# A gated-attention kernel with routed rows: VectorE's order in a step, the place of the score transposes, gate loads, and the first chunk's M

## The chip, the cores and the metric

The kernel runs on one core of a Trainium2 chip. A core has five engines that run side by side, each with its own queue in program order: TensorE (PE in the profile; PEld are its weight loads), VectorE (DVE), ScalarE (ACT), GpSimd (POOL) and SyncE (SP), which here only issues DMAs. TensorE writes into PSUM; VectorE and ScalarE read it there. The metric is the device time of one execution in microseconds, as the median over runs.

## The reference

Two blocks, one behind the other. The first is an mLSTM cell over four batches, eight heads, 768 time steps and 40 elements to a head; the second picks 128 of the 768 rows of each batch by a score and sends them through a two-layer network.

```python
for t in range(S):                                   # per batch and head
    m_new = max(f[t] + m, i[t])
    C = exp(f[t] + m - m_new) * C + exp(i[t] - m_new) * outer(v[t], k[t])
    n = exp(f[t] + m - m_new) * n + exp(i[t] - m_new) * k[t]
    m = m_new
    y[t] = sigmoid(o[t]) * (C @ q[t]) / max(abs(n @ q[t]), 1)
x = y as rows of 320                                 # heads side by side
scores = x @ w_gate
top = the 128 rows of a batch with the largest scores
out[top] = x[top] + sigmoid(scores[top]) * (relu(x[top] @ w1) @ w2);  out elsewhere = x
```

## The kernel before

**Chunks and steps.** The time steps of a batch are cut into six chunks of 128, so there are 24 steps, numbered n = 0 to 23; step n treats chunk c = n mod 6 of batch b = n div 6. Within a chunk the recurrence becomes matrix products: scores of keys with queries (`pS`), multiplied by decay weights (`W`) to give `P`, and `P` times the values (`pH`); the state `C` from the chunks before contributes through `pIC`. The order on every engine is the order in which the program writes the operations (a manual schedule); waits for data and for free buffers are added to it.

**The gates.** The sums of f and the running maxima M are made for three chunks at a time (group g = 0 and 1) on 96 rows: `sums`, `maxima`, `ends` (three matmuls `pe`), `carry` (the state m from chunk to chunk), `carried` (three matmuls `pm`), `level` (M with the carried m), `scales` (`wk`, `r`) and `columns`/`keep` (`pc`, `cols`). M and a are each split into three bf16 parts (`split`), from which `operands(u, c)` builds, for the batches 2u and 2u+1 and chunk c, two operands: six small matmuls into two PSUM tiles `pO`, then `a_o` by ScalarE and `M_o` either by VectorE (`beside=True`, one operation) or by ScalarE (four operations). `weights` multiplies the two (`pW`) and takes the exponential to give `W`; `causal` masks W on GpSimd.

**A step.** `step(n)` issues, in this order: the loads of chunk n + 4; `within(n)` (`pH`); `exchange(n + 1)` (`pIC`), `decay` (GpSimd) and `products(n + 1)` (`pS`); `weights(n + 2)`; `norm` (VectorE adds `pH` to `num` and makes the denominators `den` and `rec`; GpSimd makes `sor`); `compare(n - 1)` (VectorE, `ge`); `result` (VectorE: `x`, and `scr`, which sums the score into `sc`; the store of x); fillers (`warm`) or the layers of the network; `turned(n + 2)` (transposes `pt`, copied to `T` by ScalarE); `gated` (ScalarE, tanh and add on `so`); `causal` and `stated` (`wv`) on GpSimd; `spread(n)` (transpose `pb` of the score just made, copied to `sb` by ScalarE); in some steps `operands`; and last `weighted(n + 1)` (VectorE, `P`) and `exchanged(n + 1)` (VectorE, `num` and `C`). In the first steps the order differs a little: W is made for other chunks, and the second group of gates is worked off between.

**What is shared.** PSUM is tight. `pt` and `pW` (and, in the changed kernel, `pg`) share two buffers; `pb`, `pO`, `pe`, `pm`, `pc` and the tiles of the ranking and the network share two; `pH` and the fillers `pw` share one; `pIC` has one.

**Ranking.** From `compare` come counts of how many rows of a batch have a larger score; in the next batch's first step they become ranks and a selection, in its second the chosen rows are gathered, and from its third on they go through the two layers.

**Loads.** k, q, v and o of a chunk are four DMAs of 160 KB on SP's queue into one of five sets of buffers. Their padding columns are written once at the start (`pads`).

## Time and profile before

| | |
|---|---|
| median of 14 runs | 203.68 us (201.86 to 205.34) |
| profiled execution | 203.21 us |
| its span | 201.5 us |
| TensorE busy, weight loads | 180.3 us (90%), 147.2 us (73%) |
| VectorE, ScalarE, GpSimd busy | 143.9, 103.6, 99.6 us (71%, 51%, 49%) |
| DMA | 24.37 MB, 121 GB/s over the span |

The span runs from the first to the last instruction that the profile shows; the profiled execution's own time is 1.71 us longer. Busy time of an engine that others wait for is what counts; idle time elsewhere costs nothing. TensorE's busy time can contain slow stretches: the profile gives the granted clock for each stretch.

### The profile page before, as it was taken

The numbers are of one execution on the slowest core, as the hardware profiler recorded it, in microseconds if no ns is written. First come the engines' busy times: TensorE is split into PE (matmuls) and PEld (weight loads), VectorE is DVE, ScalarE is ACT, GpSimd is POOL, SyncE is SP. The second block draws the span as 40 slices with busy tenths as digits, with TensorE's granted clock in tenths as the row PEclk, the third lists the DMA queues.
The fourth block names the chain that finished last, engine by engine and source line by source line (L and its number), as shares of the span: only waits on it lengthen the run. The fifth ranks groups of instructions, "written<-read, shape, count | busy, mean of one in ns | idle before, by whom it ended". The sixth has DMA issues, their size and how long they took to land.

```text
span 201.5 us, 6516 instructions
## 1 busy us (share of the span) xinstructions
PE 180.3 (90%) x2597; PEld 147.2 (73%) x2606; DVE 143.9 (71%) x418; ACT 103.6 (51%) x245; POOL 99.6 (49%) x148
## 2 busy tenths in 40 slices
PE   6988979969779779799999999899999998998990
PEld 2556858856648648698988789788887897978970
DVE  7649997867477667578688689967886899576101
ACT  5684467794784685664644445456445554201110
POOL 7149708526296375426555766266557661122201
PEclk9999999997999999999999999999999999999999
DMA  4999999999969999977899679778993101010100
GB/s 81 108 171 142 157 173 162 187 224 123 207 135 145 218 172 202 160 125 108 125 146 159 125 127 153 126 131 108 150 135 80 37 33 36 33 37 29 36 0 33
DMA packets 105854, 24.37 MB, mean 121 GB/s; under 512 B 100640, under 2 KB 105248, under 8 KB 105824
## 3 DMA queue, kind: packets, MB, share of 16 engines
q1 hardware_dynamic: 105296, 22.60, 73.9%
q0 software_dynamic: 384, 1.31, 2.0%
q8 instruction: 20, 0.33, 0.8%
q14 instruction: 10, 0.08, 0.2%
q10 hardware_dynamic: 144, 0.05, 0.1%
HBM read 19.37 MB, written 4.59 MB: 119 GB/s over the span
## 4 chain that ended last, share of the span: by engine, by line
PE 51%; DVE 19%; issue 9%; ACT 7%; DMA 5%; SPq 4%; POOL 3%; POOLq 1%
PE pH L385 11%; PE pS L328 8%; PE pt L286 6%; PE ph L496 5%; PE pIC L354 5%; PE py L505 3%; ACT T L287 3%; DVE P L334 3%; PE pIC L360 3%; PE pW L306 3%; POOL sor L400 3%; PE pw L178 3%; DVE scr L408 3%; DVE x L405 2%; SPq L93 2%
## 5 line engine op out<-in xcount | busy, mean ns | idle before, releaser
L400 POOL TENSOR_TENSOR sor<-so,rec 128x320 f32<-128x320 f32 x24 | 23.4, 976 | 47.8 <-DVE rec L398 46.3
L307 ACT ACTIVATE W<-pW 128x512 f32<-128x512 f32 x48 | 26.1, 596 | 39.4 <-PE pW L306 15.5
L312 POOL TENSOR_SCALAR_AFFINE_SELECT W<-W 128x512 f32<-128x512 f32 x48 | 33.2, 715 | 16.6 <-ACT W L307 16.2
L287 ACT COPY T<-pt 128x512 f32<-128x512 f32 x48 | 26.0, 591 | 18.7 <-PE pt L286 18.6
L334 DVE TENSOR_TENSOR P<-pS,W 128x512 f32<-128x512 f32 x48 | 30.7, 679 | 0.8 <-POOL W L312 0.8
L385 PE MATMUL pH<-v,P 128*64 128x64 f32 x768 | 28.7, 228 | 1.4 <-DVE P L334 1.4
L385 PEld LDWEIGHTS pH<-v,P 128*64 128x64 f32 x768 | 25.2, 139 | 5.3 <-DVE P L334 2.4
L328 PE MATMUL pS<-T 64*128 64x128 f32 x384 | 28.1, 286 | 0.0
L286 PE MATMUL pt<-ident,qk 128*128 128x128 f32 x192 | 25.7, 275 | 0.3 <-DMA qk<-in_q_dram 0.3
L286 PEld LDWEIGHTS pt<-ident,qk 128*128 128x128 f32 x192 | 21.9, 141 | 5.0 <-ACT W L307 1.3
L328 PEld LDWEIGHTS pS<-T 64*128 64x128 f32 x384 | 23.5, 189 | 1.5 <-issue 0.2
L496 PE MATMUL ph<-xeT,w 128*128 128x128 f32 x192 | 23.8, 280 | 0.0
L496 PEld LDWEIGHTS ph<-xeT,w 128*128 128x128 f32 x192 | 22.1, 192 | 1.7 <-issue 1.6
L392 DVE TENSOR_TENSOR num<-num,pH 128x328 f32<-128x328 f32 x20 | 9.9, 496 | 18.3 <-PE pH L385 18.2
L405 DVE TENSOR_TENSOR x<-num,sor 128x320 f32<-128x320 f32 x20 | 11.9, 594 | 10.3 <-POOL sor L400 10.3
L505 PE MATMUL py<-w,hT 128*128 128x320 f32 x64 | 19.1, 440 | 0.0
L319 POOL TENSOR_TENSOR wv<-v,cols 128x328 f32<-128x328 f32 x20 | 15.0, 751 | 5.1 <-DVE cols L260 5.1
L354 PE MATMUL pIC<-C,T 128*64 128x82 f32 x320 | 15.8, 242 | 0.8 <-DVE C L377 0.8
L421 DVE SCALAR_TENSOR_TENSOR ge<-sb,sc,earlier 128x128 bf16<-128x128 f32 (+5 forms) x23 | 16.5, 715 | 0.0
L408 DVE CUSTOM_DVE_ANT_0 scr<-x,wg 128x320 f32<-128x320 f32 x24 | 14.6, 608 | 0.8
L354 PEld LDWEIGHTS pIC<-C,T 128*64 128x64 f32 x320 | 13.2, 141 | 2.2 <-issue 1.7
L247 ACT ACTIVATE M_o<-pO,of_which,which 128x128 bf16<-128x128 f32 x36 | 13.5, 457 | 2.2 <-PE pO L236 1.4
(131 smaller groups left out, 260.4 us busy)
## 6 DMA issues: line engine op xcount, KB each, us to landing
qk<-in_k_dram SPq DMA_DIRECT2D x24, 160.0 KB, 3.8
qk<-in_q_dram SPq DMA_DIRECT2D x24, 160.0 KB, 4.6
v<-in_v_dram SPq DMA_DIRECT2D x24, 160.0 KB, 4.9
so<-in_o_gate_dram SPq DMA_DIRECT2D x24, 160.0 KB, 4.8
out_dram<-x SPq DMA_DIRECT2D x24, 160.0 KB, 1.9
w<-in_moe_w_dram SPq DMA_DIRECT2D x2, 640.0 KB, 4.4
w<-in_moe_w_dram SPq DMA_DIRECT2D x2, 512.0 KB, 3.8
w<-in_moe_w_dram SPq DMA_DIRECT2D x1, 256.0 KB, 3.9
```

What stands on the lines that cost most here:

```text
L286: nc.tensor.transpose(pt[:, p, :], qk[:, j, 2 * p:2 * p + 2, :].rearrange("s a d -> s (a d)"), ident)
L287: nc.scalar.copy(out=T[:, j], in_=pt)
L307: nc.scalar.activation(out=W[:, h0:h0 + 4, :], in_=pW, func=AF.Exp)
L312: nc.gpsimd.affine_select(out=W[:, h0:h0 + 4, :], in_=W[:, h0:h0 + 4, :], compare_op=OP.is_ge, fill=0.0, base=0, pattern=[[0, 4], [1, L]], ...
L328: nc.tensor.matmul(pS[j][:, p, :], T[e, 0, p, :], T[e, 1, p, :], start=True, stop=True)
L334: nc.vector.tensor_tensor(out=P[:, :, j, :], in0=pS[j], op=OP.mult, in1=W.rearrange("p (n a) t -> p n a t", a=2)[:, :, j, :])
L354: nc.tensor.matmul(pI[t, 2 * p * D1:2 * (p + 1) * D1], T[:, 1, p, t], C[:, p].rearrange("e a d -> e (a d)"), start=True, stop=True)
L385: nc.tensor.matmul(pH[t, 2 * p + j, :], P[:, p, j, t], v1[:, 2 * p + j, :], start=True, stop=True)
L400: nc.gpsimd.tensor_tensor(out=sor, in0=so, in1=rec.unsqueeze(2).to_broadcast([128, H, D]), op=OP.mult)
L408: nc.vector.tensor_tensor_reduce(out=scr, in0=x, in1=wg, scale=1.0, scalar=0.0, op0=OP.mult, op1=OP.add, accum_out=sc[:, c:c + 1])
L496: nc.tensor.matmul(self.ph[:, f % 4, :], w1[:, j, f * 128:(f + 1) * 128], self.xeT[:, j, :], start=(j == 0), stop=(j == NDC - 1))
L505: nc.tensor.matmul(self.py, self.hT[:, f, :], w2[:, f, :], start=(f == 0), stop=(f == NFC - 1))
```

## The change

1. **Order of VectorE in a step.** Behind the denominators come `exchanged(n + 1)` and `weighted(n + 1)` (in step 0 `weighted` first), ahead of `compare` and `result`. `weights`, `causal` and `stated` for chunk n + 2 and the layers follow `norm` in the program; `gather` stands behind the layers, `columns_of` and the entry of the layers behind the transposes.
2. **Scores a step later.** `spread(n - 1)` and `compare(n - 1)` are both issued in step n: spread behind the transposes and ahead of `gated`, compare behind `result`. In a batch's first step (and in the last step of all) spread comes right behind `pS` and compare ahead of `result`.
3. **Operands.** `operands` stands at the end of a step, in steps 1 and 2 for the chunks 4 and 5, in steps 3 to 8 for the second pair of batches. Where `beside` is false the two `pO` tiles are one.
4. **Gate loads.** Each of the four gate tensors is one DMA instead of three; three of them are on ScalarE's queue. The row `w_gate` is loaded once (1 x 320) and spread to 128 rows by a matmul with a column of ones (`pg`), instead of a 160 KB DMA.
5. **First chunk's M.** Before the first chunk there is no state, so the running maximum needs no carry there: the three parts of M for chunk 0 are made from it at once, on 32 rows, and `operands(0, 0)` uses them; `level` and the split of all 96 rows follow.
6. **Start.** `pH(0)` is issued before step 0, ahead of the second half of chunk 1's transposes, `pW(1)` and `pIC(0)`. Padding columns of chunks 0 and 1 are written by ScalarE, those of 2, 3 and 4 by GpSimd; a's first split moves to GpSimd; the second group's sums and maxima stand ahead of the state's copy.

```diff
     def load_gates(eng, dst, src, g):
-        for c in range(3):
-            t = slice((3 * g + c) * L, (3 * g + c + 1) * L)
-            eng.dma_start(out=dst[g][c * BH:(c + 1) * BH], in_=src[:, :, t].rearrange("b h p -> (b h) p"))
+        t = slice(3 * g * L, 3 * (g + 1) * L)
+        eng.dma_start(out=dst[g], in_=src[:, :, t].rearrange("b h (c p) -> c (b h) p", p=L))
...
-        pO = [ps_m.tile([128, L], FP, name=f"pO{j}", tag="m") for j in range(2)]
+        if beside:
+            pO = [pool.tile([128, L], FP, name=f"pO{j}", tag=tag) for j in range(2)]
+        else:
+            both = pool.tile([128, 2, L], FP, name="pO", tag=tag)
+            pO = [both[:, j] for j in range(2)]
...
+        soon = n > 0 and (c == 0 or n == N - 1)
         if n + 1 < N:
+            decay(*steps[n + 1])
+            if n == 0:
+                pS[n + 1] = products(T[n + 1])
             give = exchange(*steps[n + 1], loaded[n + 1][0], T[n + 1], wv[n + 1])
-            decay(*steps[n + 1])
-            pS[n + 1] = products(T[n + 1])
-        if 1 < n < NT - 2:
-            operands(0, n + 2, beside=False)
-        if n + 2 < N and not late:
-            W[n + 2] = weights(*steps[n + 2])
+            if n > 0:
+                pS[n + 1] = products(T[n + 1])
+        if soon:
+            pb, pc = steps[n - 1]
+            spread(pc, *state[pb][1][:2])
 
         num, sor = norm(nums.get(n), pH, so)
...
-        if n > 0:
-            pb, pc = steps[n - 1]
+        if n == 0:
+            P[n + 1] = weighted(pS[n + 1], W[n + 1])
+        if n + 1 < N:
+            nums[n + 1] = exchanged(*steps[n + 1], *give)
+        if 0 < n < N - 1:
+            P[n + 1] = weighted(pS[n + 1], W[n + 1])
+        if soon:
             compare(pc, *state[pb][1])
         if c == 0:
             state[b] = open_batch()
-        result(b, c, num, sor, state[b][0])
...
+        run(more.get("weights", ()))
+        if n + 2 < N:
+            if n != 1:
+                stated(n + 2)
+            W[n + 2] = weights(*steps[n + 2])
+            causal(W[n + 2])
+        layer(b, c)
+        if b > 0 and c == 1:
+            picked[b - 1] = gather(b - 1, number(sel[b - 1], token))
+        if n + 2 < N:
+            turned(n + 2)
...
+        if n > 0 and not soon:
+            pb, pc = steps[n - 1]
+            spread(pc, *state[pb][1][:2])
         if n + 2 < N:
-            turned(n + 2)
             gated(n + 2)
...
+        result(b, c, num, sor, state[b][0])
+        if n > 0 and not soon:
+            compare(pc, *state[pb][1])
...
+        if n in (1, 2):
+            operands(0, n + 3, beside=False)
+        elif 3 <= n < 3 + NT:
+            operands(1, n - 3, beside=False)
```

and at the start (the hooks of steps 0 and 1 are listed where they are passed):

```python
    def second_operands():
        split(1, 1, nc.gpsimd)
        operands(0, 2, beside=False)
        ends(1)

    def level_and_split():
        level(1, kept["pm"])
        scales(1)
        split(1, 0, nc.vector)

    def more_operands():
        operands(0, 3)
        kept["pc"] = columns(1)

    step(0, pH=pH, carry=[sums_and_state], weights=[second_operands], end=[lambda: carry(1), second_places])
    step(1, carry=[lambda: kept.update(pm=carried(1))], sor=[level_and_split], weights=[more_operands],
         end=[lambda: keep(1, kept["pc"])])
```

## The prediction

> **What bounds the kernel now.** I read the page's busy times first, then the list of waits, then timelines at TensorE's longest gaps, then windows of one microsecond for the granted clock.

> ```profile
> PE 180.3 (90%) x2597; PEld 147.2 (73%) x2606; DVE 143.9 (71%) x418; ACT 103.6 (51%) x245; POOL 99.6 (49%) x148
> ```

> ```profile
> DVE num L392 <- PE pH L385: 18.2, 14, 2.7
> ...
> DVE x L405 <- POOL sor L400: 12.1, 20, 0.6
> ...
> PE pO L236 <- ACT sb L415: 6.6, 5, 1.7
> ...
> PE pH L385 <- DVE P L334: 1.4, 4, 0.5
> ```

> TensorE is busy 90% of the span, so only its idle time and its slow-clock time can be won. VectorE waits for TensorE (18.2 us for pH), while TensorE waits for P only 1.4 us in all. The diff's main idea, P earlier, therefore attacks a wait that hardly exists. The large entry is pO waiting for ScalarE's copy of sb. One such place, from the timeline (start, duration, engine, line, tiles, in brackets the idle time before):

> ```profile
> 50.73 0.27 PE L414 MATMUL pb<-ident,sc 128*128 128x128 f32 x1
> ...
> 50.94 0.34 PE L236 MATMUL pO<-a,placea 32*128 32x128 bf16 x3
> ...
> 51.41 0.47 ACT L297 ACTIVATE so<-so 128x320 f32<-128x320 f32 x1
> 51.92 0.47 ACT L298 ACTIVATE so<-so 128x320 f32<-128x320 f32 x1
> 52.29 0.25 ACT L415 COPY sb<-pb 128x128 f32<-128x128 f32 x1
> 52.59 0.32 PE L236 MATMUL pO<-M,placeM 32*128 32x128 bf16 x3 [1.32 <-ACT sb L415]
> ```

> pb and the two pO tiles share two PSUM buffers. The second pO needs pb's buffer, and pb's copy stands on ScalarE behind tanh and add. TensorE stops for 1.32 us, and pH of the next step stands behind it. Steps 3, 4, 5, 7 and 8 show 1.65, 1.32, 0.90, 1.32 and 1.37 us, 6.56 in sum. After the longest the clock falls (last three columns: clock, DMA share, GB/s):

> ```profile
> 42.00:43.00 1.00, 0.02 (x1) 0.00 (x0) 1.00 (x3) 0.97 (x3) 0.00 (x0) 1.00 0.82 204
> ...
> 44.00:45.00 1.00, 1.00 (x26) 1.00 (x28) 0.00 (x0) 0.96 (x3) 0.00 (x0) 0.69 1.10 292
> 45.00:46.00 1.00, 1.00 (x14) 0.48 (x10) 0.39 (x1) 0.54 (x2) 0.00 (x0) 0.50 1.47 178
> 46.00:47.00 1.00, 1.00 (x16) 0.96 (x16) 0.90 (x5) 0.81 (x2) 0.09 (x1) 0.50 1.54 136
> 47.00:48.00 1.00, 1.00 (x14) 0.82 (x14) 0.39 (x3) 0.27 (x1) 1.00 (x2) 0.61 1.55 136
> ```

> In the chain of waits pH takes 1.57 there instead of 1.08, pW 0.54 instead of 0.32, pIC 1.29 instead of 1.02, pS 1.30 instead of 1.09: 1.2 us lost.

> **The change, part by part.** I call the stretch from pH(n) to pH(n+1) step n. In the chain pH starts at 15.54, 22.11, 29.86, 35.69, 44.00, 52.91, 59.75, 67.49, 74.91 and 82.49 us for n = 0 to 9.

> *Front, up to pH(1).* The gate loads leave SP's queue (six issues, 4.78 to 8.22), so chunk 1's k and q are issued 3.5 us sooner, 4.4 with f's two issues saved ahead of them, and their wait of 0.33 at 12.84 goes. The row of wg replaces a 160 KB load and costs TensorE one matmul (a py matmul of that width has a pitch of 0.29) and ScalarE one copy (at most 0.59, the T copy), both under other waits. The f gates land about 3.1 (issue 0.81 plus a median of 2.2), two scans and a subtraction (0.42, 0.43, 0.29) end at 4.3, the four splitting operations of 32 rows (0.20 to 0.29) at 5.3. M no longer waits for carry and level, so the first pO end at 7.8 instead of 8.8, M_o (0.75) at 8.55, W's exponentials (0.55 each) and masks (0.61) at about 11.2, and pH(0) starts near 12.4: 3.1 earlier. That is then handed back. pW(1), the second half of chunk 1's transposes and pIC(0) used to stand ahead of pH(0) and now stand behind it. From pH(0)'s end at 13.5: pW(1) 13.9, its exponential and the transposes and copy for q 15.2, pS(1) 16.3, pIC(1) 17.4, six pO and pe 18.3. Next on TensorE is pW(2), which needs M_o(0,2); ScalarE makes it after those pO (0.37 plus 4 x 0.375 pitch), at 19.9. TensorE waits 1.6. Then pW, fillers and transposes: pH(1) at 22.2. **+0.1**, ends -0.7 and +1.3 (gate landing 0.5 either way, POOL's masks and splits at slow sizes).

> *Step 1.* Now pW(3) stands behind pO(0,3), and VectorE makes M_o(0,3) only after P(2). From pH(1)'s end: num to rec 1.06, level 0.15 + 0.85 + 0.07, the whole split 0.98 (it was cut in two), num and C 0.40 + 0.65, P 1.25, M_o 0.75: 6.16. With pH 1.15 that is 7.3, while TensorE has run out of work at 5.2 (pIC 1.05, pS 1.09, then pO held by the split, pc 0.43). It waits 2.1, and behind it stand pW 0.35, fillers 0.65, transposes 0.87, pb 0.2 and pO(0,4) 0.45: 9.8 us instead of 7.75. **+2.05**, ends +1.4 (level's maximum at 0.28, as in the first group, not 0.81) and +2.1. So in this step P is not right behind the denominators. Step 2 gains nothing: 5.9 for 5.83, **+0.1**.

> *Steps 3 to 8.* pb now carries the score of a step ago and its copy stands ahead of tanh and add, and the operand matmuls use one tile instead of two. The five gaps go (6.56), the 0.21 in which pb waited for sc, and the clock loss (1.2). Six pO (0.45) and one pair of pW (0.35) were extra in steps 3 and 4 and are now in steps 1 and 2, counted there. **-8.77**. What is late next is ScalarE: W 1.08, T 1.07, sb 0.25, tanh and add 0.95, a_o and M_o 1.87 make 5.2 of a step of 5.6 to 6, so it just fits. DMA covers itself: loads are issued four steps ahead, and a load takes under 5 us.

> *Step 6, the first chunk of batch 1.* There num is pH itself, so the fillers, which share pH's only buffer, wait until x has read it:

> ```profile
> 61.40 0.97 DVE L421 SCALAR_TENSOR_TENSOR ge<-sb,sc,earlier 128x768 bf16<-128x768 f32 x1
> 61.57 1.39 POOL L400 TENSOR_TENSOR sor<-so,rec 128x320 f32<-128x320 f32 x1 [0.66 <-DVE rec L398]
> ...
> 62.99 0.49 DVE L405 TENSOR_TENSOR x<-pH,sor 128x320 f32<-128x320 f32 x1 [0.61 <-POOL sor L400]
> ...
> 63.74 0.81 PE L178 MATMUL pw<-earlier 128*128 128x512 bf16 x2
> ```

> Now num (0.40), C (0.65), P (1.25) and the comparison (0.9) stand ahead of x. Counted from pH's start, pS ends at 3.35, P at 4.6, the comparison at 5.55, x at 6.1; pW is done at 3.9: the fillers wait 2.2, and transposes and the next pH wait behind them. The old waits of 1.18 and 0.14 go. **+0.9**.

> *VectorE behind P.* x, scr and the comparison now run where POOL masks W and scales v. x takes 0.49 or 0.90 in this trace, scr 0.49 or 0.80. VectorE's busy time in steps 3 to 8 is 32.8 us, TensorE's work after the change 38, so most of this is covered; if it were not, x and scr at slow size in each step cost 0.7. **+0.5**, ends 0 and +2.5. In exchange sor runs beside num, C and P. It takes 0.72 beside a 128-wide comparison, 1.19 beside a 640-wide one.

> [...]

> *Clock.* Three new waits stand at 1.6, 2.1 and 2.2 us. In this trace 1.65 was followed by half clock and 1.37 was not. I take slightly more than one such fall at 1.2 us, **+1.4**, ends 0 and +3.6.

> [...]

> *Steps 9 to 23 and the tail.* TensorE's own waits here are 0.17, 0.53, 0.38, 0.17, 0.53 and 0.39, 2.2 in sum, all on VectorE's P or C, and P is now ready about 1.5 us before it is needed. I take **-1.2**, ends 0 and -2.0, because idx now waits on VectorE for a pidx that stands behind the py matmuls. The tail's work is the same.

> Sum: 0.1 + 2.05 + 0.1 - 8.77 + 0.9 + 0.5 + 1.4 - 1.2 = -4.92. The profiled execution took 203.21 (span 201.5 and 1.71 around it), so 198.29; the median of the runs is 0.47 above it, so **198.8**.

> **Rivals.** *The front costs nothing more than it must* (chance 0.17): all terms at their lower ends, -0.7 + 1.4 + 0.1 - 8.77 + 0.9 - 2.0 = -9.1, 194.6. For it: VectorE's busy time has 1 us of room per step. *The new waits eat the gain* (0.17): front +1.3, step 1 +2.1, three clock falls 3.6, VectorE 0.5, late steps 0: 1.3 + 2.1 + 0.1 - 8.77 + 0.9 + 0.5 + 3.6 = -0.3, 203.4, about half of it still inside 'faster'. *VectorE becomes the bound* (0.16, slower): x, scr and the comparison, last in its queue, are held by POOL in every step. Busy time 5.47 a step (32.8 / 6), x +0.41, scr +0.31, the comparison +0.54 (half of what 1.65 against 0.57 for 384 columns shows): 6.73. It decides from 6.66, the mean of steps 3 to 23 (139.8 / 21). Then 21 x 0.07 = 1.5 lost, nothing of the gaps won, and the front's 2.25 stays: 207.4. Against it: slow sizes are already in the 5.47.

> **Chances.** My forecast has 0.50, and all of it is faster. A difference below 0.5% (1.0 us) can't be told from none here. Faster 0.50 + 0.17 + 0.08 = 0.75, same 0.09, slower 0.16. The range runs from the first rival's time to just past the second's, 194.6 to 204.3; it leaves out the slower rival and little else.

> **What would show it.** Right: no pO waits on sb; pW waits 1.6 on ScalarE's M_o in step 0 and 2.1 on VectorE's M_o in step 1; pH(2) near 32, pH(3) near 38, then steps of 5.6 to 6.2; in step 6 fillers wait about 2.2 on x; pH(9) near 79. Wrong: pH(2) before 30 or after 34; half clock in more than two stretches; pH waiting for P from step 9 on, which means VectorE binds; steps 9 to 23 changed by over 3 us either way.

## The result: 216.0 us, slower by about 5%

The changed kernel took 215.99 us as the median of 10 runs (211.74 to 217.79) against 203.53 of 47 runs of the kernel before: the ratio is 1.049, with a 95% interval of 1.044 to 1.054. The prediction was 198.8, faster. The profiled execution took 214.55 us (span 212.8), 11.3 more than the one of before and 16.3 more than the sum of the prediction gave.

Executions of one and the same kernel lie up to 8.8 us apart and show different mean clocks (203.35 to 212.13 us and 0.929 to 0.973 in the run with both loads mended), so a ratio compares the least disturbed executions of both kernels, and where none is given the medians and ranges stand alone.

### The profile page after: what moved, and what is told of

The parts are those of the page before. It is cut to its first block, busy times and chain, and to the rows that moved or that the text cites. A ratio compares the mean times of both kernels' runs of the same rounds, so it can differ in the third digit from the quotient of the medians.

```text
span 212.8 us, 6502 instructions
## 1 busy us (share of the span) xinstructions
PE 189.5 (89%) x2598; PEld 155.2 (73%) x2607; DVE 146.8 (69%) x417; ACT 104.2 (49%) x242; POOL 99.9 (47%) x158
## 4 chain that ended last, share of the span: by engine, by line
PE 67%; DMA 12%; issue 7%; ACT 5%; DVE 5%; ACTq 1%; POOLq 1%; POOL 1%
PE pH L388 12%; PE pt L289 11%; PE pS L331 10%; PE ph L499 8%; PE pIC L357 5%; PE py L508 5%; DMA xe<-out_dram,idx 5%; PE pW L309 4%; PE pIC L363 4%; PE pw L179 3%; DMA v<-in_v_dram 3%; DMA wg_row<-in_moe_w_gate_dram 2%; PE pO L239 2%; ACT T L290 2%; DMA out_dram<-ye,idx 1%
## 5 line engine op out<-in xcount | busy, mean ns | idle before, releaser
L315 POOL TENSOR_SCALAR_AFFINE_SELECT W<-W 128x512 f32<-128x512 f32 x48 | 36.0, 773 | 24.6 <-ACT W L310 24.6
L403 POOL TENSOR_TENSOR sor<-so,rec 128x320 f32<-128x320 f32 x24 | 17.8, 740 | 51.9 <-DVE rec L401 40.6
L289 PE MATMUL pt<-ident,qk 128*128 128x128 f32 x192 | 29.8, 303 | 0.7 <-ACT W L310 0.7
L388 PE MATMUL pH<-v,P 128*64 128x64 f32 x768 | 30.1, 237 | 0.0
L289 PEld LDWEIGHTS pt<-ident,qk 128*128 128x128 f32 x192 | 24.4, 155 | 6.7 <-ACT W L310 4.0
L388 PEld LDWEIGHTS pH<-v,P 128*64 128x64 f32 x768 | 26.7, 148 | 3.6 <-issue 1.6
L424 DVE SCALAR_TENSOR_TENSOR ge<-sb,sc,earlier 128x128 bf16<-128x128 f32 (+5 forms) x23 | 16.9, 736 | 17.4 <-ACT sb L418 16.9
L179 PE MATMUL pw<-earlier 128*128 128x512 bf16 x29 | 12.7, 494 | 4.7 <-DVE x L408 2.2
L411 DVE CUSTOM_DVE_ANT_0 scr<-x,wg 128x320 f32<-128x320 f32 x24 | 16.1, 669 | 0.9
L508 PEld LDWEIGHTS py<-w,hT 128*128 128x128 f32 x64 | 11.5, 191 | 5.0 <-issue 1.4
L514 POOL DMA_INDIRECT out_dram<-ye,idx x4 | 4.6, 1143 | 20.1 <-DVE ye L512 20.1
```

Source lines behind the costliest of these rows:

```text
L179: nc.tensor.matmul(pw, earlier[:, 0:128], earlier[:, 0:4 * L], start=True, stop=True)
L289: nc.tensor.transpose(pt[:, p, :], qk[:, j, 2 * p:2 * p + 2, :].rearrange("s a d -> s (a d)"), ident)
L315: nc.gpsimd.affine_select(out=W[:, h0:h0 + 4, :], in_=W[:, h0:h0 + 4, :], compare_op=OP.is_ge, fill=0.0, base=0, pattern=[[0, 4], [1, L]], ...
L388: nc.tensor.matmul(pH[t, 2 * p + j, :], P[:, p, j, t], v1[:, 2 * p + j, :], start=True, stop=True)
L403: nc.gpsimd.tensor_tensor(out=sor, in0=so, in1=rec.unsqueeze(2).to_broadcast([128, H, D]), op=OP.mult)
L508: nc.tensor.matmul(self.py, self.hT[:, f, :], w2[:, f, :], start=(f == 0), stop=(f == NFC - 1))
```

## The profile after

From the page, busy times and the clock row (40 slices of 5.3 us each; 9 is full clock):

```profile
PE 189.5 (89%) x2598; PEld 155.2 (73%) x2607; DVE 146.8 (69%) x417; ACT 104.2 (49%) x242; POOL 99.9 (47%) x158
...
PEclk9755969658999966999999999999999999999999
```

TensorE has one instruction more and is busy 9 us longer. The clock row gives the reason: before, one slice was below 9; now there are nine. I added up 1 minus the clock over windows of one microsecond: 17.1 us lost after, 1.7 before. The stretches are 8 to 22 us (6.8 lost), 28 to 32 (1.7), 38 to 50 (5.1) and 76 to 84 (3.4). In the windows the last three columns are clock, DMA share and GB/s, the first behind the length is TensorE:

```profile
10.00:11.00 1.00, 1.00 (x4) 0.68 (x4) 0.00 (x0) 0.43 (x1) 0.00 (x0) 0.50 1.20 177
20.00:21.00 1.00, 1.00 (x24) 1.00 (x22) 0.93 (x3) 0.37 (x1) 1.00 (x2) 0.50 1.55 136
42.00:43.00 1.00, 1.00 (x7) 1.00 (x6) 0.00 (x0) 0.46 (x1) 0.22 (x1) 0.50 1.19 211
```

TensorE is busy in all three: work is there, and it runs at half speed.

The list of waits (us in all, times, longest) has the entries of the prediction:

```profile
DVE num L395 <- PE pH L388: 8.2, 4, 4.1
...
PE pW L309 <- DVE M_o L245: 2.3, 1, 2.3
...
PE pw L179 <- DVE x L408: 2.2, 1, 2.2
...
PE pW L309 <- ACT M_o L250: 1.6, 1, 1.6
...
PE pO L239 <- ACT sb L418: 0.6, 1, 0.6
...
DVE x L408 <- POOL sor L403: 0.6, 1, 0.6
```

pO waits 0.6 us for sb instead of 6.6, x 0.6 for sor instead of 12.1, and the three new waits of 1.6, 2.3 and 2.2 us are where they were put. A steady step shows the mended place: pb, both pO and the copy sb in one go, with sb ahead of tanh (timeline, end of step 3):

```profile
58.03 0.27 PE L417 MATMUL pb<-ident,sc 128*128 128x128 f32 x1
...
58.24 0.34 PE L239 MATMUL pO<-a,placea 32*128 32x128 bf16 x3
...
58.41 0.33 PE L239 MATMUL pO<-M,placeM 32*128 32x128 bf16 x3
...
58.71 0.27 ACT L418 COPY sb<-pb 128x128 f32<-128x128 f32 x1
...
58.87 0.48 ACT L300 ACTIVATE so<-so 128x320 f32<-128x320 f32 x1
```

Waits in the front that were not foreseen, and the issue of the row of wg (timeline, idle time before in brackets):

```profile
3.78 0.55 ACTq L93 DMA_DIRECT2D wg_row<-in_moe_w_gate_dram  x1
...
5.31 0.42 DVE L183 TENSOR_TENSOR_SCAN FM<-earlier,f_sb 96x128 f32<-96x128 bf16 x1 [2.68 <-DMA f_sb<-in_f_gate_dram]
...
6.71 0.32 PE L193 MATMUL pe<-FM,ident 96*32 96x2 f32 x6 [2.37 <-POOL a L219]
...
8.96 0.90 PE L651 MATMUL pg<-wg_row,one 1*128 1x320 f32 x1 [1.39 <-DMA wg_row<-in_moe_w_gate_dram]
```

The wait in step 1, and one in step 8 that was not foreseen:

```profile
39.66 0.61 PE L309 MATMUL pW<-M_o,a_o 32*128 32x512 bf16 x2 [2.35 <-DVE M_o L245]
...
93.56 0.55 PE L479 MATMUL pX<-ident,xe 128*128 128x128 f32 x3 [1.21 <-DMA xe<-out_dram,idx]
```

Starts of pH(n) by the timelines, in us, for the runs that the text leans on:

| n | 0 | 1 | 2 | 3 | 6 | 9 | 23 |
|---|---|---|---|---|---|---|---|
| before | 15.47 | 22.04 | 29.79 | 35.62 | 59.68 | 82.42 | 175.39 |
| after | 19.68 | 32.20 | 44.92 | 52.73 | 69.53 | 95.09 | 186.10 |
| after, wg by DMA | 16.93 | 31.62 | 44.35 | 50.30 | 67.09 | 88.53 | 179.54 |
| after, both loads mended | 14.84 | 26.41 | 39.14 | 46.92 | 63.71 | 88.69 | 179.70 |
| after, fillers in the front | 16.16 | 26.39 | 39.65 | 47.61 | 64.40 | 90.70 | 181.71 |
| after, M_o(0,3) early | 19.61 | 31.77 | 41.98 | 49.33 | 66.12 | 91.97 | 184.91 |
| after, fillers in step 1 | 19.00 | 30.62 | 41.61 | 47.56 | 64.35 | 90.54 | 181.55 |
| after, no fillers in step 6 | 19.39 | 31.93 | 44.26 | 50.21 | 67.00 | 86.52 | 177.52 |
| before, P first alone | 15.47 | 22.04 | 29.78 | 37.28 | 63.13 | 88.90 | 191.69 |
| before, spread late alone, mended | 16.08 | 23.14 | 30.77 | 37.59 | 56.64 | 83.18 | 183.01 |
| before with mended steps | 15.37 | 22.44 | 30.06 | 36.51 | 55.03 | 77.72 | 170.37 |
| after with four mends | 12.73 | 23.79 | 33.45 | 39.39 | 56.19 | 77.25 | 168.26 |

By the table the changed kernel loses 17.1 us up to pH(3), wins 7.3 back in steps 3 to 5, loses 2.8 between pH(6) and pH(9), and wins 1.4 from there to the end of the span.

## The experiments

My theory ("clock"): each short wait of TensorE starts a stretch of half clock that costs as much as the wait or more. The rival ("late data"): only the waits themselves cost, and the slow clock goes along with them.

### The front

*Gates of the first group in three DMAs each, as before.*

```diff
-    load_gates(nc.sync, f_sb, f_gate, 0)
-    load_gates(nc.scalar, i_sb, i_gate, 0)
+    load_thirds(nc.sync, f_sb, f_gate, 0)      # the loop of before
+    load_thirds(nc.scalar, i_sb, i_gate, 0)
```

> The changed kernel with the first group's f and i gates loaded in three DMAs each again. In its trace the scan of f waits until 5.31 us for its load, pH(0) starts at 19.75 and TensorE runs at half clock from 8.4 to 21.6. Theory 'clock': the 1.8 us of earlier data do not help by themselves, because TensorE still waits for wg_row's row (8.96) and still falls to half clock: within 1 us of 216. Theory 'late data': everything in the front moves up by what f lands earlier, 5.31 to about 3.5: 214.

Median 212.24 (208.88 to 215.35, 4 runs; the changed kernel 211.74 to 217.79). The scan starts at 3.5 instead of 5.31 and TensorE's wait ahead of pe falls from 2.37 to 0.56, but now pg waits 3.74 for the row of wg, which still lands at 9.5:

```profile
9.51 0.90 PE L656 MATMUL pg<-wg_row,one 1*128 1x320 f32 x1 [3.74 <-DMA wg_row<-in_moe_w_gate_dram]
```

One late load had stood behind the other; pH(1) is at 30.80 instead of 32.20. The median lies below what either theory expected (216 and 214), but the ranges overlap, so a gain in the total is not established.

*The row of wg as a 160 KB broadcast DMA behind chunk 1's k, q, v and o; no pg.*

```diff
-    wg_row = const.tile([1, DM], FP, name="wg_row")
-    nc.scalar.dma_start(out=wg_row, in_=...)
...
     load(1)
+    nc.sync.dma_start(out=wg, in_=<moe_w_gate, 128 times>)
...
-    pg = ...; nc.tensor.matmul(pg, one, wg_row, ...); nc.scalar.copy(out=wg, in_=pg)
```

> The changed kernel with w_gate spread over the partitions by a 160 KB DMA on SP's queue again, and no pg matmul. The wait of 1.39 us before pg goes, the wait of 2.4 us before pe (for f) stays. Theory 'clock': with one idle stretch of 2.4 us instead of 2.4 and 1.4 the clock may hold or fall later; if it holds until pH(0), about 6 us faster (210), if it still falls, 215. Theory 'late data': 1.4 us faster, 214.6.

Median 208.40 (206.39 to 209.09, 4 runs), ratio to before 1.026 (1.015 to 1.036), clear of the changed kernel's 1.044 to 1.054 and lower than either theory expected. In the profiled execution little of it comes from the front, where pH(1) stands at 31.62 for 32.20 and the transposes still take 1.06 to 1.12, the pace of half clock (four take 0.66 with the fillers below). Most comes later: step 2 takes 5.95 instead of 7.81, and steps 6 to 8 take 21.44 instead of 25.56, because here no half clock follows the wait of 2.16 in step 6 (mean clock of the execution 0.980, in the changed kernel's 0.920).

*Both.*

> The changed kernel with the first group's gates in three DMAs each and w_gate by a 160 KB DMA, so both waits of the front are undone. Theory 'clock': no idle stretch over 1 us is left ahead of pH(0), the clock stays full, pH(0) starts near 12.5 and pH(1) near 23 to 24: 207 to 209. Theory 'late data': 1.8 + 1.4 = 3.2 us faster, 212.8.

Ratio 1.002 (0.998 to 1.007); the median of 12 runs is 208.89 over 203.35 to 212.13, the widest spread of all. By the ratio the two late loads, with what follows them, are worth nearly all of the 5%; by the medians, 7.1 of 12.5 us. The median is where "clock" put it (207 to 209), but not for its reason: it expected full clock ahead of pH(0), pH(0) near 12.5 and pH(1) at 23 to 24. In the profiled execution these stand at 14.84 and 26.41, and the first transposes take 1.11, the pace of half clock, though from 2 us to 13 TensorE waits no longer than 0.57. Half clock then follows from 22 to 27, 33 to 44 and 70 to 78 us (mean clock of the execution 0.944).

*Late data kept, clock held: fillers in the front.*

```diff
-    warm(6)
+    warm(12)
...
-    warm(2)
+    warm(7)
     split(0, 0, nc.vector, slice(0, BH))
```

> The changed kernel with eleven more filler matmuls in the front: 12 instead of 6 ahead of pe and 7 instead of 2 ahead of pg. No data come earlier; TensorE is only kept busy while it waits. Theory 'clock': the granted clock stays full from about 5 us on, pH(0) starts near 15 instead of 19.75, pH(1) near 25 instead of 32.3: 208 to 210, although work was added. Theory 'late data': no gain, 216, or slower by what the fillers overrun.

Median 211.35 (210.15 to 213.42, 4 runs), between what the theories expected (208 to 210, and 216); ratio 1.045 (1.035 to 1.055): in the total not separable from the changed kernel, in the front it is. The scan still starts at 5.3, yet pH(0) stands at 16.16 instead of 19.68 and pH(1) at 26.39 instead of 32.20. Three runs below change nothing ahead of pH(1); there it stands at 30.62, 31.77 and 31.93. So 11 matmuls that do nothing won 4.2 to 5.8 us. The same four transposes, first in the changed kernel, then with fillers:

```profile
10.32 1.11 PE L289 MATMUL pt<-ident,qk 128*128 128x128 f32 x4
```

```profile
9.65 0.66 PE L289 MATMUL pt<-ident,qk 128*128 128x128 f32 x4
```

Rival "late data" gives this gain no place. One thing stays open: the changed kernel has 6 fillers ahead of pe where the kernel before has 8, and no run puts back those two alone.

### Steps 1 and 6

*M_o(0,3) ahead of num, C and P on VectorE.*

```diff
         split(1, 0, nc.vector)
+        operands(0, 3)
     def more_operands():
-        operands(0, 3)
```

> The changed kernel with one thing moved: in step 1 the operands of chunk 3 are issued right behind the split of M, so on VectorE M_o(0,3) stands ahead of num, C and P instead of behind P. The 2.35 us that TensorE waits for M_o there goes; P(2) is 0.75 us later, for which there is room. Theory 'clock' (a gap of TensorE starts a half-clock stretch, and the stretch costs more than the gap): the stretch from 38 to 50 us goes or shrinks as well, so 216.0 falls by 4 to 7 us, to 209 to 212. Theory 'late data' (only the waits themselves cost): 216.0 falls by 2.4 us at most, to 213.6.

Median 213.97 (206.73 to 214.98, 4 runs): unclear in the total, and by the median nearer to "late data" (213.6) than to "clock" (209 to 212). The wait is 0.45 instead of 2.35, and pH(1) to pH(3) takes 17.56 us instead of 20.53. Half clock falls there all the same, from 38 to 46 us for 38 to 50, although no wait near its start is longer than 0.45. In the profiled execution a further stretch of half clock, from 89 to 97 us, which the changed kernel's did not have, took most of the gain back.

*The wait kept, ten fillers in it.*

```diff
         operands(0, 3)
         kept["pc"] = columns(1)
+        warm(10)
```

> The changed kernel with ten filler matmuls (0.21 us each at full clock) put between pc and pW(3) in step 1. The wait of 2.35 us for M_o(0,3) stays as long as it is, but TensorE works through it. It does nothing but hold the clock. Theory 'clock': the half-clock stretch from 38 to 50 us goes, about 5 us less, 216.0 falls to 210 to 212. Theory 'late data': nothing is won, 215.5 to 216.5.

Median 210.42 (205.44 to 211.12, 4 runs); all four lie below the fastest execution of the changed kernel, and the median is in the 210 to 212 of "clock". pH(1) to pH(3) takes 16.94 instead of 20.53, with 27 to 31 and 71 to 79 as the only slow stretches that the windows show:

```profile
35.80 2.10 PE L179 MATMUL pw<-earlier 128*128 128x512 bf16 x9
38.09 0.39 PE L309 MATMUL pW<-M_o,a_o 32*128 32x512 bf16 x2 [0.19 <-DVE M_o L245]
```

pW(3) starts 2.68 us behind the last pc, as in the changed kernel (36.98 to 39.66), and takes 0.39 instead of 0.61. The wait is as long as it was; what was won, 3.6 us between these two executions, came from the clock. In five other executions that leave steps 1 and 2 as they are in the changed kernel, pH(1) to pH(3) takes 18.28 to 21.22, so the gain is 1.3 us at least.

*No fillers in step 6.*

```diff
             else:
-                warm(3)
+            elif b == 0 or c > 0: warm(3)
```

> The changed kernel without the three fillers in step 6, which share pH's buffer and wait 2.16 us for x there. The transposes behind them no longer wait for x. Theory 'clock': the wait and the half-clock stretch from 76 to 84 us (3.4 us lost) both go, 216.0 falls by 4 to 6 us, to 210 to 212. Theory 'late data': only the wait and the fillers' 0.65 us go, at most 2.8 us, 213.2; less where the transposes then wait for W's exponentials.

Median 207.36 (206.01 to 210.56, 4 runs), ratio 1.020 (1.005 to 1.035), clear of the changed kernel's interval. pH(6) to pH(9) takes 19.52 instead of 25.56, 6.0 us less: the wait of 2.16, the fillers' 0.65, the half clock from 76 to 84, and the wait of 1.21 for the gathered rows in step 8, which is not there either. Both theories had expected a smaller gain (210 to 212, and 213.2). The transposes now wait for W instead:

```profile
71.57 1.15 PE L289 MATMUL pt<-ident,qk 128*128 128x128 f32 x8 [0.73 <-ACT W L310]
```

The two profiled executions differ by 8.3 us; the other 2 or so lie in steps 1 and 2, almost all in step 2, whose code is the same and where the slow stretch (39 to 43 us, for 38 to 50) was shorter in this execution.

### Parts of the change alone, on the kernel before

*The steps of the change, front of before.*

```diff
+        if soon: spread(n - 1)                    # first chunk of a batch, last step
         num, sor = norm(nums.get(n), pH, so)
+        if 1 < n < N - 1:
+            nums[n + 1] = exchanged(...); P[n + 1] = weighted(...)
...
             turned(n + 2)
+        if n > 0 and not soon: spread(n - 1)
             gated(n + 2)
-            spread(n)
...
-        if n + 1 < N:
+        if n < 2:
             P[n + 1] = weighted(...); nums[n + 1] = exchanged(...)
+        if n > 0 and not soon: compare(n - 1)     # last in the step
```

> The kernel before with only the steps changed, its front and gate loads untouched: from step 2 on num, C and P stand right behind the denominators, the score transpose and comparison of a step ago are issued behind the transposes, and pO is one tile where ScalarE makes M_o. Theory 'the steps are right, the front is what lost': the five waits of pO for sb (6.6 us) and the clock loss of 1.2 us go, step 6 gives 0.9 and a half-clock stretch of up to 3.4 us back: 203.5 falls to 195 to 199. Rival 'the new order of a step loses too' (x, scr and the comparison held by GpSimd, or step 6's wait): 202 or more.

Median 207.60 (206.34 to 210.65, 5 runs), ratio 1.017 (1.006 to 1.027): slower, as the rival had it (202 or more). But I had left the matmuls that sum the comparisons (pcol) in their old place, ahead of the layers and transposes, and this made three waits. One of them, from TensorE's timeline of step 12, with the transposes of the step before for comparison:

```profile
98.45 1.04 PE L290 MATMUL pt<-ident,qk 128*128 128x128 f32 x8
...
105.96 0.72 PE L432 MATMUL pcol<-ones_b,ge 128*128 128x1 bf16 x21 [2.60 <-DVE ge L425]
106.55 3.55 PE L509 MATMUL py<-w,hT 128*128 128x320 f32 x6
109.89 1.92 PE L290 MATMUL pt<-ident,qk 128*128 128x128 f32 x8
```

The same eight transposes take 1.92 instead of 1.04, the clock reads 0.50 from 105 to 111 us, and step 12 took 12.2 us.

*The same with pcol behind the transposes, as in the changed kernel, and no fillers in step 6.*

```diff
-        if b > 0 and c == 0: pcol = columns_of(...)
...
             turned(n + 2)
+        if b > 0 and c == 0: pcol = columns_of(...)
```

> The kernel before with the steps of the change (order of VectorE, score transposes a step later, one pO tile), with the sums of the comparisons behind the transposes as in the changed kernel, and without the fillers of step 6. The front and the gate loads are those of before. Theory 'clock': the three waits of 2.60 us for the comparison in steps 6, 12 and 18 of the run with the steps alone, and the half-clock stretch of 3.4 us behind each, go, and the wait in step 6 too: 203.4 falls to 190 to 194. Rival 'the steps lose time of their own': 198 or more.

Median 198.38 (198.10 to 201.01, 6 runs), ratio 0.981 (0.974 to 0.988): faster than before, but 4 us short of what "clock" expected, and at the bound that I gave the rival. Both hold in part. Step 12 takes 7.0 us, so the wait of 2.60 had cost 5.2, half of it by the clock. And the steps lose a little of their own: from pH(2) to pH(6) they take 24.97 us, in the changed kernel with four mends 22.74, and pIC waits here for GpSimd's wv, an entry that the other's list of waits lacks (us, times, longest):

```profile
PE pIC L364 <- POOL wv L323: 4.3, 4, 1.3
```

*The main idea alone: P first, scores spread and compared as before.*

```diff
         num, sor = norm(nums.get(n), pH, so)
+        if 1 < n < N - 1:
+            nums[n + 1] = exchanged(...); P[n + 1] = weighted(...)
```

> The kernel before with the main idea alone: from step 2 on num, C and P stand right behind the denominators, ahead of the comparison and x. Spread and comparison stay in their places of before. What the order would break is put out of the way: the 21 matmuls that sum the comparisons stand behind the transposes, and step 6 has no fillers. Theory 'P was never late': TensorE waited 1.4 us for P in all and 2.2 us for P or C from step 9 on, so 203.4 falls by 1 to 3 us, to 200.5 to 202.5. Rival 'P first makes the score late': x and with it the score come about 2 us later, pb and the copy sb too, so pO waits longer for sb, in steps 3 to 8 by 1 us each or more: 204 to 210.

Median 223.05 (219.52 to 224.89, 4 runs), ratio 1.101 (1.093 to 1.109). The rival's cause held, the late score, at far more than its price (204 to 210) and at another matmul than it named: pO waits only 1.0 us for sb, the wait has moved to pb. From the list of waits:

```profile
PE pb L414 <- DVE sc L408: 10.4, 11, 2.0
...
PE pb L414 <- ACT so L297: 4.1, 3, 1.5
```

x and the score come later by num, C and P; pb, which transposes that score in the same step, stands on TensorE ahead of the next pH and waits for it.

*The score transposes a step later alone.* The diff is that of the steps without the lines of num, C and P; the comparison stands behind P.

> The kernel before with the score transposes alone: from step 1 on spread of a step ago is issued behind the transposes and ahead of tanh and add, its comparison last in the step on VectorE, and pO is one tile where ScalarE makes M_o. VectorE's P stays behind x, scr. Theory 'the waits of pO for sb were the gain': the five waits (6.6 us) and the clock loss (1.2 us) go, 203.4 falls to 195 to 197. Rival 'the gain needs P earlier too': steps 3 to 8 then wait for P instead, 199 to 203.

Median 210.29 (209.17 to 211.54, 4 runs), ratio 1.034 (1.026 to 1.041), with the same three waits of pcol. So the run was made again with pcol behind the transposes:

> The kernel before with the score transposes a step later and one pO tile as in the run with the spread alone, and with the sums of the comparisons behind the transposes, so that TensorE doesn't wait for the comparison in steps 6, 12 and 18. VectorE's P stays behind x and scr. Theory 'the waits of pO for sb were the whole gain': 203.4 falls to 196 to 198.5, as in the run with the mended steps. Rival 'the spread alone wins nothing, P must come earlier too': 201 or more, with pH waiting for P in the trace.

Median 210.26 (209.53 to 212.84, 6 runs), ratio 1.035 (1.027 to 1.044): the rival holds. Steps 3 to 5 do win 5.0 us (19.05 from pH(3) to pH(6), before 24.06), so pO's waits go. But in a batch's first step x stands behind a comparison that now waits for its copy, and elsewhere P stands behind x and scr:

```profile
PE pH L389 <- DVE P L338: 4.3, 4, 1.3
...
PE pw L178 <- DVE x L409: 3.0, 1, 3.0
```

The fillers of step 6, which the run with the mended steps left out, are still in this one. Their wait of 3.0 and the half clock behind it lie in steps 6 and 7, which take 4.5 us more than before. But from pH(9) to the end, where they have no part, this run takes 126.2 us for 119.1 before, and that alone is more than the 5.0 won.

Neither half pays by itself. P first makes the score late; spreading a step later makes a late score harmless. Together, without the waits beside them, they win 2%.

### Towards a faster version

*All four mends in the changed kernel: gates in thirds, wg by DMA, M_o(0,3) early, no fillers in step 6.*

> The changed kernel with all four mends: gates of the first group in three DMAs each, the row of wg as one broadcast DMA behind chunk 1's loads instead of a matmul, M_o(0,3) ahead of num and P in step 1, no fillers in step 6. Theory 'clock': both waits of the front, those of steps 1 and 6 and the half-clock stretches behind them go; what stays of 216.0 is the wait of 1.6 us in step 0 and the one of 1.2 us in step 8: 196 to 200. Theory 'late data': the sum of the waits taken away, 1.9 + 1.4 + 2.35 + 2.16 + 0.65 = 8.5 us, 207.5.

> The run with the four mends again, beside the one with chunk 2's operands early, on the same chip: 196 to 200 as before.

Median 198.35 (196.34 to 199.54, 4 runs), ratio 0.979 (0.971 to 0.986); again 197.51 (196.14 to 200.22, 6 runs), ratio 0.969 (0.964 to 0.975). "Late data" expected 207.5, "clock" 196 to 200. The wait of 1.2 us in step 8, which "clock" had expected to stay, is gone too: among the changed kernel and the runs made from it, it shows in the six executions in which half clock followed the fillers' wait of step 6, and in no other is it over 0.2 us. The clock row of the first:

```profile
PEclk9999799999999799999999999999999999999997
```

So the waits alone do not account for the loss; with the clock behind them the sum comes out. But "each" in my theory is too strong. Counted over the profiled executions of the changed kernel and of the runs made from it, half clock follows the wait of 1.57 us in step 0 in 9 of 10, that of 2.35 in step 1 in 6 of 6, and that of 2.16 in step 6 in 6 of 7; the clock lost behind one and the same wait lies between 1.7 and 5.1 us. What decides whether and how long is not shown.

In the clock row above two slices are left, beside the very last. One follows the wait of 1.57 us in step 0, which I tried to remove in two ways.

*pW(2) behind the fillers and transposes.*

> The changed kernel with all four mends and a fifth: in step 0 pW(2) stands behind the fillers and chunk 2's transposes, so that TensorE works through the 1.57 us that it waits there for ScalarE's M_o. Theory 'clock': the wait and the half-clock stretch from 21 to 26 us (1.7 us) go, 198.4 falls by 2 to 3.3 us, to 195 to 196.5. Theory 'late data' (the wait moves: T's copy and then W's exponentials come later on ScalarE and P(2) in step 1 is late instead): 198 to 199.

Median 201.11 (199.09 to 202.58, 12 runs), ratio 0.987 (0.982 to 0.992): no gain over the run with four mends. The wait moved, as the rival said, though to another place and at a higher price than it named (198 to 199). In step 0 the fillers share pH's buffer as in step 6, and now came up first; from the list of waits:

```profile
PE pw L181 <- DVE x L410: 1.1, 1, 1.1
```

Step 0 takes 10.3 us, less than with four mends (11.1 and 11.4), but step 1 takes 11.1 instead of 9.7 and 9.3, and half clock falls from 32 to 40 us.

*The operands of chunk 2 ahead of step 0.*

> The changed kernel with all four mends, and the operands of chunk 2 issued ahead of step 0, behind the tanh of chunk 1, instead of inside it, so that ScalarE has made M_o(0,2) before TensorE asks for it (1.57 us in the run with four mends). Theory 'clock': the wait and the half-clock stretch of 1.7 us behind it go and nothing new waits: 2 to 3.3 us less than the run with four mends beside it, 195 to 196.5. Rival, as when pW(2) was moved back: ScalarE or VectorE is late elsewhere in the front, no gain or a loss, 198 to 201.

Median 196.71 (194.08 to 198.01, 6 runs), ratio to before 0.963 (0.957 to 0.968), the best of the study. Step 0 takes 9.5 us instead of 11.4, and the fillers wait 1.17 for x here too. Beside the run without this edit (197.51, its interval overlaps) the gain is not established.

## Why the prediction was wrong

The forecast's mechanism for the steady part held. Two steps of it failed: the front's loads, which it took to come early or to be covered by other waits, and the price of the clock behind a wait. Two of its own signs of being wrong came: pH(2) at 44.92, where 34 was the limit, and half clock in four stretches instead of at most two. Measured against the prediction's own terms, in the profiled execution:

| stretch | predicted | measured |
|---|---|---|
| front, up to pH(1) | +0.1 | +10.2 |
| step 1 | +2.05 | +5.0 |
| step 2 | +0.1 | +2.0 |
| steps 3 to 8 | -8.77 + 0.9 | -4.4 |
| VectorE behind P, clock | +0.5, +1.4 | inside the stretches |
| step 9 to the end | -1.2 | -1.4 |

The misses are 10.1, 2.9, 1.9 and 3.4 less 0.2 and less the 1.9 that had no place: 16.2 of the 16.3 us.

**Front, the f gates' landing: wrong.** "The f gates land about 3.1 (issue 0.81 plus a median of 2.2)" took the 2.2 us of a 16 KB DMA for a 48 KB one. The scan started at 5.31, 2.2 us later than that. Nor did chunk 1's k and q come 3.5 to 4.4 us sooner: they were issued at 6.15 and 8.52, before at 8.27 and 8.74, because two of the issues ahead of q's took 2.3 and 2.5 us.

**Front, the row of wg: wrong.** I costed it at nothing, "under other waits", and looked only at its matmul and copy. Its DMA stood fourth on ScalarE's queue, was issued at 3.78 and landed at 8.92. The row of 1.2 KB took 5.1 us from its issue, as long as the 160 KB loads beside it (median of k 4.4, q 5.2, v 5.5). pg stands in TensorE's order ahead of the first transposes, so TensorE stood still for 1.39 us.

**Front, the rest: nearly right.** With early gates and no pg, pH(0) stood at 12.73 in the first run with four mends; predicted 12.4. In the second, the same code, it stood at 14.83, because the front ran at the pace of half clock to about 13 us (four transposes in 1.11 instead of 0.66). The wait of 1.6 us for M_o(0,2) measured 1.58.

**Clock: the term that was mis-sized.** I took "slightly more than one such fall at 1.2 us" and at most three. There were four stretches, of 13.6, 3.4, 10.2 and 6.8 us (twice the clock that each lost). The last three follow the waits of 1.58, 2.35 and 2.16 that I had placed, so taking the 1.65 us row for waits of this length was right here; the first and longest lies behind the two waits of the front that I had not seen. What failed was the length of one: I took it from the only row there was. Fillers show the price: 4.2 us or more in the front, 1.3 or more in steps 1 and 2; and in step 12 a wait of 2.60 cost 5.2. The second rival had three falls in it and came out at 203.4, too low for the same reason, and the range with it.

**Step 1 and step 2.** The wait was 2.35 for a predicted 2.1. At the end of step 1 pO still waits 0.63 for sb, which the forecast had put at nothing. The rest of the miss, and all that step 2 missed, is half clock from 38 to 50 us.

**Steps 3 to 8.** In steps 3 to 5 the gain was 7.3 us (16.80 from pH(3) to pH(6), before 24.06), with steps of 5.94, 5.49 and 5.37 against a predicted 5.6 to 6.2. Step 6's wait was 2.16 for 2.2. What followed it was missing from the sum: half clock from 76 to 84, and the wait of 1.21 for the gathered rows in step 8, which is over 0.2 us only where half clock followed the fillers' wait.

**VectorE behind P.** sor fell to a mean of 740 ns from 976, x rose to 644 from 594 and scr to 669 from 608: 0.11 us a step, and no pH waits for P. sor takes 0.72 us in 23 of its 24 executions after, 22 of them beside num, C or P; beside a comparison it took up to 1.39 before. x (from num and sor) takes up to 0.90 us and scr up to 0.80 while GpSimd masks W, 0.48 to 0.49 where GpSimd does nothing beside them. No run shows the 2 us more in the term's upper end, +2.5; the runs showed the 0.11 us a step.

**"Attacks a wait that hardly exists": right, and not the point.** P first alone lost 10%. It pays only together with the later score transposes, which make its late score harmless.

**The slower rival** named the wrong mechanism: VectorE's busy time in the whole span is 146.8 of 212.8, and no pH waits for P. That a slower outcome had a chance of 0.16 is no credit to the forecast: what lost, the front and its clock, stood in no rival at more than a fraction of its size.

## What to carry to other kernels

Price a new wait on TensorE at its length plus, as a likely term, a stretch of half clock (here 21 of 23 waits of 1.57, 2.35 and 2.16 us had one behind them, with 1.7 to 5.1 us of clock lost), and look for work that can stand in it: ten idle matmuls in step 1's wait, which was as long as ever, won at least 1.3 us. Compare several executions before a stretch of half clock is put down to one wait. Take a DMA's landing time from a row of its own size and place in its queue: here about 4.5 us for 48 KB, a median of 2.2 for 16 KB, 5.1 for 1.2 KB behind three loads. Before a part of a change is judged, ask which other part makes room for it: here P first alone lost 10%, the later transposes alone 3.5%, both together won 2%.

## What the runs showed of the hardware

Where an execution began at the pace of half clock, the clock row did not show it. In the run with wg by DMA the first two pS took 2.08 us each and the first pH 1.98 (1.16 and 1.15 in the run with fillers in the front), while six windows between 7 and 27 us show 1.00; there the durations of equal matmuls tell it. So it is with the first fillers, under a clock of 1.00 too: eight take 3.59 us before, six 2.74 after, while nine take 2.10 in the run with fillers in step 1. I therefore take the 17.1 and 1.7 us counted above as lower bounds.

The load of 48 KB in one DMA landed about 4.5 us after its issue (issued at 0.81, the scan that waits for it starts at 5.31), 16 KB ones from the same tensor after a median of 1.7 us (three, in the run with both loads mended) and 2.2 (six, before).
